# New slots and engines for the elementwise work of an attention-plus-Mish block

## The chip, the cores and the metric

The kernel runs on one core of a Trainium2 chip. The metric is the device time of one execution in microseconds (us), lower is better. Before the change it is 1112.99 us, the median of three runs (1112.70 to 1113.39).

The engines of a core are named as the profile does: PE is TensorE (matmuls; PEld is its weight load), DVE is VectorE, ACT is ScalarE, POOL is GpSimd, and SP issues the transfers (DMAs). Each engine runs its own instructions in program order and waits at semaphores for the others.

## The reference

```python
def _A_ref(x, wqkv, wo):          # S=2048 tokens, D=576, 32 heads of 18
    q, k, v = ...                 # x @ wqkv
    idx = pos[:, None] - (jnp.arange(8) * 2)[None, :]   # 8 keys: the token and every second before it
    logits = jnp.einsum("bhsd,bhswd->bhsw", q, kg) * scale
    attn = _softmax(jnp.where(mask, logits, -1e9), axis=-1)
    o = jnp.einsum("bhsw,bhswd->bhsd", attn, vg)
    return o.transpose(...).reshape(B, S, D) @ wo

def _B_ref(x, w1, b1, w2):        # F=4608
    h = jnp.einsum("bsd,df->bsf", x, w1) + b1
    act = h * jnp.tanh(stable_softplus(h))               # Mish
    return jnp.einsum("bsf,fd->bsd", act, w2)

xn = _layernorm(x)
return x + _A_ref(xn, A_wqkv, A_wo) + _B_ref(xn, B_w1, B_b1, B_w2)
```

Everything is float32. The attention is a sliding window of eight dilated keys, so it has no large matmul: its products of queries with keys and of weights with values are elementwise.

## The kernel before

The 2048 tokens are worked in two halves of 1024 (`hf` 0 and 1). A half goes through these matmul stages on TensorE: the layernormed tokens transposed (`ta`, `tb`), the query-key-value product (`pq`, L424, and the `z` items, L594), for each of 18 blocks of the hidden width the first MLP product with Mish (`h`, L826 and L832, in six parts), and the second MLP product (`po`: L948 in the first half, as products named P1 to P7 by L1084 and L1100 in the second). At the end comes the output product (`o`, L1230). Every float32 operand is split into two pieces, "high" (a rounded copy, mostly made by ScalarE) and "low" (the difference, an elementwise subtraction), and a product takes three matmuls: high·high, high·low, low·high. The matrices are also multiplied in schemes of seven products in place of eight on 2×2 blocks, which need sums and differences of blocks ahead (`tt`, `S`, `ra`, `rm`, `v`, `wa`), each split into high and low again. This is the elementwise work that fills VectorE and GpSimd:

- low parts: `t`, `w`, `wa`, `wc`, `wq` (L271), `u` and `ud` (L1007), `act` (L893), `v` (L384);
- block sums: `w1_sum` `tt` (L256), `v_sum` (L376), `wa` (L302), `u_sum` (L994);
- taking results out of PSUM, which GpSimd never reads: `h` in L882, `acc` in L952, `accP` in L1106, `zqs` in L607;
- the attention (L677 and on): a half has 8 pairs (`n` is half_pair). For each pair `pr` = query times window of keys (L699), VectorE reduces it (L704), softmax (L714 to L730), `pv` = weights times values (L737), VectorE reduces it into `og` (L743), and the last reduce's result is stored. Each `pr` and `pv` product comes as two instructions of 128×576, with the keys `pr half_pair k c x` and `pv half_pair k h x`. `pr` and `pv` share one tag of two buffers.

The order of all work is written out by hand. A list of TensorE items, `plan`, gives the rows of a timeline, six slots to an item; matmuls stand in slot 4. Every piece of elementwise work and every transfer is put into the slot that `before` or `soon` work out from the item that it is for, moved by a table of numbers:

```python
def put(pos, fn, key):
    pos += MOVE.get(key, 0)
    assert pos > now[0], key
    timeline[pos].append(fn)

def engine(default, *key):
    k = " ".join(str(x) for x in key)
    return nc.vector if k in ON_VECTOR else nc.gpsimd if k in ON_GPSIMD else default
```

The attention runs as a generator, one step of it in each slot named `att n`. The timeline is then gone through slot by slot, and the instructions of each engine are chained in that order. So three tables decide, for each engine, which instruction stands behind which: `MOVE` (how many slots earlier or later), `ON_VECTOR` and `ON_GPSIMD` (which engine, where it is not the default). `pr` and `pv` are GpSimd's by default; the low parts of L271 VectorE's; those of `u` some of each.

## Time and profile before

| what | value |
|---|---|
| median of 3 runs | 1112.99 us (1112.70 to 1113.39) |
| the profiled execution, its own time | 1111.6 us |
| its span in the profile | 1109.7 us |
| granted TensorE clock | 1.000 |
| busy: PE, DVE, POOL, ACT | 1088.6, 976.2, 770.8, 532.8 us |
| moved by DMA | 290.51 MB, 262 GB/s mean |

The span runs from the first instruction to the last. The 1.9 us between it and the execution's own time lie outside what the profile shows. Busy times of engines overlap. "A <- B" in the view of waits means that A stood idle until B was done.

### The profile page before, as it was taken

How to read it: one execution, taken by the hardware profiler on the slowest of the kernel's cores; microseconds unless marked ns; L12 is line 12 of the kernel's file. 1: busy time of each engine (PE TensorE's matmuls, PEld its weight loads, DVE VectorE, ACT ScalarE, POOL GpSimd, SP SyncE). 2: the span in 40 equal slices, each digit the busy share in tenths (PEclk: the TensorE clock that was granted, in tenths of full speed). 3: DMA queues.
4: the chain of work that ended last, by engine and by line, in shares of the span. 5: the costliest groups of instructions: out<-in, count | busy, mean ns of one | idle time of the engine just before them, and what ended most of it. 6: DMA issues, size and time to landing. Idle time of an engine off the chain costs nothing.

```text
span 1109.7 us, 18409 instructions
## 1 busy us (share of the span) xinstructions
PE 1088.6 (98%) x6414; PEld 993.4 (90%) x6414; DVE 976.2 (88%) x1580; ACT 532.8 (48%) x984; POOL 770.8 (69%) x595
## 2 busy tenths in 40 slices
PE   8999999999999999999999999999999999999998
PEld 7898999899989988799999888888988899989998
DVE  7843899998998988998877899999999999998886
ACT  5644656546555545863233364354444344434332
POOL 5342668785677878768657477776988878896652
PEclk9999999999999999999999999999999999999999
DMA  8698999897799879877597798557565668675772
GB/s 272 220 334 260 326 317 310 280 326 261 268 315 340 313 284 359 302 232 270 183 313 242 252 357 270 197 205 236 184 233 188 253 213 298 223 265 179 276 224 93
DMA packets 171377, 290.51 MB, mean 262 GB/s; under 512 B 32242, under 2 KB 107284, under 8 KB 171284
## 3 DMA queue, kind: packets, MB, share of 16 engines
q1 hardware_dynamic: 171284, 289.33, 75.7%
q8 instruction: 51, 0.84, 0.3%
q14 instruction: 42, 0.34, 0.1%
HBM read 179.05 MB, written 110.23 MB: 261 GB/s over the span
## 4 chain that ended last, share of the span: by engine, by line
PE 62%; DVE 16%; POOL 9%; issue 5%; ACT 4%; DMA 3%; SPq 0%; POOLq 0%; DVEq 0%; ACTq 0%
PE h L826 18%; PE po L1100 9%; PE po L948 9%; PE pq L424 6%; PE z L594 6%; PE pd L1084 5%; PE o L1230 4%; PE h L832 4%; POOL pr L699 3%; POOL pv L737 2%; DVE pv L737 2%; DVE og L743 2%; POOL u L1007 1%; DVE accP L1106 1%; DVE acc L952 1%
## 5 line engine op out<-in xcount | busy, mean ns | idle before, releaser
L1100 PEld LDWEIGHTS po<-pw,u 128*128 128x128 f32 x1512 | 207.6, 188 | 13.9 <-POOL u L1007 3.1
L1100 PE MATMUL po<-pw,u 128*128 128x288 f32 x1512 | 214.2, 296 | 5.3 <-DVE accP L1106 2.0
L948 PEld LDWEIGHTS po<-w,act 128*128 128x128 f32 x1152 | 157.7, 188 | 5.5 <-DVE acc L952 1.5
L948 PE MATMUL po<-w,act 128*128 128x288 f32 x1152 | 160.8, 295 | 0.7 <-DVE acc L952 0.7
L737 POOL TENSOR_TENSOR pv<-L,kv 128x576 f32<-128x576 f32 x85 | 133.6, 1649 | 35.6 <-ACT zkv L603 9.1
L699 POOL TENSOR_TENSOR pr<-q,kv 128x576 f32<-128x576 f32 x89 | 144.7, 1644 | 13.7 <-DVE og L743 12.5
L826 PE MATMUL h<-xt,t 128*128 128x512 f32 x432 | 111.2, 393 | 2.8 <-DVE rd_raw L882 1.5
L826 PE MATMUL h<-S,t 128*128 128x512 f32 x432 | 110.6, 391 | 0.0
L826 PE MATMUL h<-xt,wa 128*128 128x512 f32 x432 | 105.3, 392 | 0.0
L1106 DVE TENSOR_TENSOR accP<-po,accP 128x288 f32<-128x288 f32 x240 | 94.8, 445 | 6.5 <-PE po L1100 6.2
L826 PEld LDWEIGHTS h<-xt,wa 128*128 128x128 f32 x432 | 81.1, 188 | 18.0
L826 PEld LDWEIGHTS h<-xt,t 128*128 128x128 f32 x432 | 79.1, 188 | 20.1 <-DVE rt L882 2.0
L424 PE MATMUL pq<-wq,xt 128*128 128x432 f32 x448 | 92.0, 361 | 1.9 <-ACT xt L96 1.1
L826 PEld LDWEIGHTS h<-S,t 128*128 128x128 f32 x432 | 78.5, 188 | 14.3 <-ACT rd_a L871 0.3
L424 PEld LDWEIGHTS pq<-wq,xt 128*128 128x128 f32 x448 | 83.0, 188 | 7.4 <-ACT xt L96 1.8
L704 DVE TENSOR_REDUCE L<-pr 128x64 f32<-128x1152 f32 x64 | 85.8, 1341 | 3.1 <-POOL pr L699 2.8
L743 DVE TENSOR_REDUCE og<-pv 128x144 f32<-128x1152 f32 x64 | 85.8, 1342 | 0.8 <-POOL pv L737 0.4
L952 DVE TENSOR_TENSOR acc<-po,acc 128x288 f32<-128x288 f32 x192 | 77.1, 446 | 10.5 <-PE po L948 10.2
L737 DVE TENSOR_TENSOR pv<-L,kv 128x576 f32<-128x576 f32 x43 | 63.0, 1495 | 0.4
L1084 PE MATMUL pd<-pd,ud 128*128 128x288 f32 x456 | 62.5, 296 | 0.0
L1084 PEld LDWEIGHTS pd<-pd,ud 128*128 128x128 f32 x456 | 61.2, 188 | 0.4 <-DVE acc L1089 0.2
L826 PE MATMUL h<-S,wc 128*128 128x512 f32 x216 | 55.8, 394 | 0.6 <-ACT c L871 0.4
(340 smaller groups left out, 2275.4 us busy)
## 6 DMA issues: line engine op xcount, KB each, us to landing
kv<-kv_d SPq DMA_DIRECT2D x64, 396.0 KB, 5.4
pw<-kept_T SPq DMA_DIRECT2D x36, 576.0 KB, 5.8
kept_t<-t SPq DMA_DIRECT2D x36, 512.0 KB, 5.5
t<-kept_t SPq DMA_DIRECT2D x36, 512.0 KB, 4.8
pw<-kept_B SPq DMA_DIRECT2D x27, 576.0 KB, 4.2
rw<-in_w SPq DMA_DIRECT2D x36, 320.0 KB, 5.0
kept_B<-w SPq DMA_DIRECT2D x36, 288.0 KB, 4.8
kept_wq<-wq SPq DMA_DIRECT2D x18, 432.0 KB, 6.0
```

Source lines behind the costliest of these rows:

```text
L424: nc.tensor.matmul(pq[:, 0:432], XT[:, xi, tok], wt[wi][:, hl, 0:432], start=i == 0, stop=i == len(seq) - 1)
L594: nc.tensor.matmul(h, l, r_, start=first and n == 0, stop=n == len(seq) - 1, skip_group_check=True)
L699: engine(nc.gpsimd, "pr", n, k, c, x).tensor_tensor(out=pr[:, x:x + hh], in0=q[:, j0 + x:j0 + x + hh, None, :].to_broadcast([P, hh, W, CU] ...
L704: nc.vector.tensor_reduce(L[:, k, j0:j0 + hj].rearrange("p j w h -> p (j w h)"), pr.rearrange("p j w (h d) -> p (j w h) d", h=2), axis=AX, ...
L737: engine(nc.gpsimd, "pv", n, k, h, x).tensor_tensor(out=pr[:, x:x + hj].rearrange("p j d w -> p j w d"), in0=L[:, k, x:x + hj, :, h:h + 1] ...
L743: nc.vector.tensor_reduce(og[:, :, c0:c0 + DH], pr, axis=AX, op=ALU.add)
L826: nc.tensor.matmul(ph, wt[:, wl, wk * P:(wk + 1) * P], X[:, xs, :], start=first and i == 0, stop=last and i == len(seq) - 1, skip_group_ch ...
L948: nc.tensor.matmul(po, acts[hf, q, b, j][:, al, tok], done["w2", hf, 2 * q + j][:, wl, c * HC:(c + 1) * HC], start=i == 0, stop=i == 5)
L952: nc.vector.tensor_tensor(out=t, in0=po, in1=t, op=ALU.add)
L1084: nc.tensor.matmul(po, units[e, k, qq][:, al, n * P:(n + 1) * P], w[qq][:, wl, :], start=i == 0, stop=i == 5)
L1100: nc.tensor.matmul(po, units[e, k, qq][:, al, tok], w[:, qq, wl, :], start=i == 0, stop=i == 5)
L1106: nc.vector.tensor_tensor(out=t, in0=po, in1=t, op=ALU.add)
```

## The change

Three lines change, all of them literal tables. `MOVE` goes from 1910 keys to 1918, and 1820 of the 1978 keys in either have another value; half of the differences are of six slots (one item) or less, the largest of 136. `ON_VECTOR` gains 106 keys and loses 77 (273 to 302), `ON_GPSIMD` gains 48 and loses 43 (145 to 150). In the diff the lines are cut to some of the keys that are spoken of below, one to a line:

```diff
 MOVE = {
...
-"act 0_1_4": 15, "act 0_1_5": 15,
+"act 0_1_4": 18, "act 0_1_5": 12,
...
-"att 60": 1, "first 1": -13, "low t0 4": -10, "low t1 3": -9, "low w2 6": -5,
+"att 60": -8, "first 1": 16, "low t0 4": -19, "low t1 3": 2, "low w2 6": -12,
...
-"u_low 1 0 0": 21, "u_low 1 0 1": -3, "u_low 1 1 0": -37, "u_low 1 1 1": 10,
+"u_low 1 0 0": 23, "u_low 1 0 1": -2, "u_low 1 1 0": -24, "u_low 1 1 1": -7,
...
 ON_VECTOR = (
...
-"pv 0_4 1 1 0", "pv 0_4 1 1 4", "pv 0_5 1 1 0", "pv 0_5 1 1 4", "pv 0_7 0 0 0", "pv 0_7 0 0 4",
-"pv 0_7 1 0 0", "pv 0_7 1 1 4", "u_low 1 2 0",
+"act 0_1_5", "pv 0_7 0 1 0", "pv 0_7 1 0 4", "u_low 1 0 0", "u_low 1 1 0", "u_low 1 1 1",
...
 ON_GPSIMD = (
...
-"low t0 4", "low t1 3", "low w2 6",
+"u_low 1 0 1",
...
```

What the tables do to the engines, by their instructions in order: TensorE has the same 6416 instructions; a group of three transposes for the output product stands one P item earlier, the rest is as before. ScalarE keeps 986 and SP its 860 transfers, in another order. VectorE goes from 1582 to 1606, GpSimd from 600 to 576. By kind, net to VectorE: −22 `pv` (11 in each half), +14 `pr` (9 and 5), +16 `u_low`, +8 `w1_sum`, +7 `t` and +4 `v_sum`, +2 `v_low`, and a few of others either way.

**First place: VectorE at the end of pair 5 of the first half's attention**, where the second half's first MLP block begins. `rt0` and `ra0` are taken from PSUM (L882). Before:

```order
L743 TENSOR_REDUCE og_0_5_7359<-pv_0_5_0_1_7425 128x8x18
L737 TENSOR_TENSOR pv_0_5_1_0_7433<-L_0_5_7157,kv1_0_11_7178 128x4x8x18
L743 TENSOR_REDUCE og_0_5_7359<-pv_0_5_1_0_7433 128x8x18
L737 TENSOR_TENSOR pv_0_5_1_1_7446<-L_0_5_7157,kv1_0_11_7178 128x4x8x18 x2
L882 TENSOR_TENSOR rt0_7407<-h3_1_0_7438,rt0_7407 128x512
L882 TENSOR_TENSOR ra0_7398<-h2_1_0_7410,ra0_7398 128x512
L743 TENSOR_REDUCE og_0_5_7359<-pv_0_5_1_1_7446 128x8x18
```

And with the change:

```order
L743 TENSOR_REDUCE og_0_5_7339<-pv_0_5_0_1_7364 128x8x18
L737 TENSOR_TENSOR pv_0_5_1_0_7399<-L_0_5_7133,kv1_0_11_7206 128x4x8x18
L302 TENSOR_TENSOR wa_1_2_7115<-wraw_1_7116,wa_1_2_7115 128x640
L743 TENSOR_REDUCE og_0_5_7339<-pv_0_5_1_0_7399 128x8x18
L882 TENSOR_TENSOR rt0_7420<-h3_1_0_7439,rt0_7420 128x512
L882 TENSOR_TENSOR ra0_7411<-h2_1_0_7423,ra0_7411 128x512
L743 TENSOR_REDUCE og_0_5_7339<-pv_0_5_1_1_7458 128x8x18
```

The last two `pv` instructions of the pair have left VectorE, and one sum `wa` has come in. At the same point of pair 4, ahead of a `zqs` evacuation, two `pv` have left too.

**Second place: VectorE between taking out the products P3 (`accP3`) and P7 (`accP7`)**, in the second half's P items, where the first half's attention pair 7 ends. Before:

```order
L737 TENSOR_TENSOR pv_0_7_0_0_8085<-L_0_7_7900,kv1_0_14_7906 128x4x8x18 x2
L882 TENSOR_TENSOR ra_r_7950<-h3_1_3_7937,ra_r_7950 128x512
...
L1106 TENSOR_TENSOR accP3_1_7485<-po_0_6_1_1_8114,accP3_1_7485 128x288
L994 TENSOR_TENSOR ra_r_7950<-ra0_7398,ra_r_7950 128x512
L743 TENSOR_REDUCE og_0_7_8084<-pv_0_7_0_0_8085 128x8x18
L1007 TENSOR_TENSOR u_1_0_1_8163<-ra_r_7950,u_1_0_1_8163 128x512
L743 TENSOR_REDUCE og_0_7_8084<-pv_0_7_0_1_8168 128x8x18
L737 TENSOR_TENSOR pv_0_7_1_0_8182<-L_0_7_7900,kv1_0_15_7935 128x4x8x18
L743 TENSOR_REDUCE og_0_7_8084<-pv_0_7_1_0_8182 128x8x18
L737 TENSOR_TENSOR pv_0_7_1_1_8186<-L_0_7_7900,kv1_0_15_7935 128x4x8x18
L1106 TENSOR_TENSOR accP7_0_7676<-po_1_0_0_0_8189,accP7_0_7676 128x288
```

And with the change:

```order
L1007 TENSOR_TENSOR u_1_1_0_7919<-rt0_7420,u_1_1_0_7919 128x512
...
L1106 TENSOR_TENSOR accP3_1_7453<-po_0_6_1_1_8106,accP3_1_7453 128x288
L882 TENSOR_TENSOR ra0_7411<-h2_1_3_7929,ra0_7411 128x512
L882 TENSOR_TENSOR ra_r_7960<-h3_1_3_7941,ra_r_7960 128x512
L994 TENSOR_TENSOR ra_r_7960<-ra0_7411,ra_r_7960 128x512
L1007 TENSOR_TENSOR u_1_0_0_8078<-rm0_7415,u_1_0_0_8078 128x512
L1007 TENSOR_TENSOR u_1_1_1_8117<-rt1_7421,u_1_1_1_8117 128x512
L743 TENSOR_REDUCE og_0_7_8066<-pv_0_7_0_0_8067 128x8x18
L737 TENSOR_TENSOR pv_0_7_0_1_8158<-L_0_7_7911,kv1_0_14_7917 128x4x8x18
L743 TENSOR_REDUCE og_0_7_8066<-pv_0_7_0_1_8158 128x8x18
L737 TENSOR_TENSOR pv_0_7_1_0_8172<-L_0_7_7911,kv1_0_15_7952 128x4x8x18
L1106 TENSOR_TENSOR accP7_0_7683<-po_1_0_0_0_8177,accP7_0_7683 128x288
```

Ahead of P3's evacuation the two `pv` and the `ra_r` evacuation have gone and a `u` stands there; between P3's and P7's, two evacuations and one `u` more, one reduce less, and `u_1_0_1` is no longer VectorE's.

**Third place: VectorE in the first half's block 2**, up to the low part `act_0_1_4` for the second MLP product. Before:

```order
L704 TENSOR_REDUCE L_0_0_1315<-pr_0_0_1_1_1675 128x64
...
L384 TENSOR_TENSOR v0_12_1651<-v0_12_1651,vh0_12_1795 128x576
L882 TENSOR_TENSOR c21_0_2_1747<-h3_0_2_1684,c21_0_2_1747 128x512
...
L336 TENSOR_TENSOR twT2_2_1734<-twT2_2_1734,twhT2_2_1897 128x576
L326 TENSOR_TENSOR twT3_3_1958<-rw2_7_1757,rw2_6_1867 128x288
L326 TENSOR_TENSOR twT3_3_1958<-rw2_6_1867 128x288
L384 TENSOR_TENSOR v2_12_1691<-v2_12_1691,vh2_12_1942 128x576
L384 TENSOR_TENSOR v3_12_1813<-v3_12_1813,vh3_12_1869 128x288
L893 TENSOR_TENSOR act_0_1_4_1901<-c21_0_2_1747,act_0_1_4_1901 128x512
```

And with the change:

```order
L384 TENSOR_TENSOR v0_12_1398<-v0_12_1398,vh0_12_1824 128x576
L271 TENSOR_TENSOR t1_0_3_1816<-tt1_3_1644,t1_0_3_1816 128x512
L704 TENSOR_REDUCE L_0_0_1281<-pr_0_0_1_1_1528 128x64
...
L893 TENSOR_TENSOR act_0_1_5_1828<-c22_0_2_1814,act_0_1_5_1828 128x512
...
L882 TENSOR_TENSOR c21_0_2_1753<-h3_0_2_1682,c21_0_2_1753 128x512
L271 TENSOR_TENSOR w2_0_6_1862<-rw2_6_1734,w2_0_6_1862 128x576
L384 TENSOR_TENSOR v2_12_1649<-v2_12_1649,vh2_12_1946 128x576
L271 TENSOR_TENSOR t0_0_4_1889<-tt0_4_1818,t0_0_4_1889 128x512
L893 TENSOR_TENSOR act_0_1_4_1943<-c21_0_2_1753,act_0_1_4_1943 128x512
```

Two `t`, a `w2` and an `act`, GpSimd's before, stand now on VectorE ahead of `act_0_1_4`, and four rows of preparation have moved elsewhere.

6 lines of the change are left out of this document (3 added, 3 removed).

## The prediction, before the changed kernel was run

> **What bounds the kernel now.** I read the engines' busy shares first. TensorE (PE) works for almost the whole span, so the time is its 1088.6 us plus what it waits: 1109.7 − 1088.6 = 21.1 us.
>
> ```profile
> span 1109.7 us, 18409 instructions
> ...
> PE 1088.6 (98%) x6414; PEld 993.4 (90%) x6414; DVE 976.2 (88%) x1580; ACT 532.8 (48%) x984; POOL 770.8 (69%) x595
> ```
>
> Since the order of TensorE's instructions hardly changes, the change can act only on those 21.1 us. Next, therefore, the view of waits for PE alone (who waited, for whom; us in total, times, longest); three rows of 0.4, 0.2 and 0.2 are left out:
>
> ```profile
> PE po L1100 <- DVE accP L1106: 2.0, 1, 2.0
> PE po L1100 <- POOL u L1007: 1.6, 4, 0.7
> PE ta L90 <- ACT xn L195: 1.5, 2, 0.9
> PE h L826 <- DVE rd_raw L882: 1.5, 1, 1.5
> PE tb L93 <- POOL rem L209: 1.4, 1, 1.4
> PE warm L80 <- POOL ident masks.py:199: 1.3, 1, 1.3
> PE pq L424 <- ACT xt L96: 1.1, 2, 0.6
> PE h L826 <- DVE rt L882: 1.1, 2, 0.7
> PE tb L91 <- DVE xt L97: 0.9, 1, 0.9
> PE po L1100 <- ACT u L1000: 0.9, 1, 0.9
> PE po L1100 <- DVE u L1007: 0.7, 1, 0.7
> PE po L948 <- DVE acc L952: 0.7, 2, 0.4
> PE z L594 <- DVE zqs L607: 0.7, 1, 0.7
> PE o L1230 <- DVE y L1234: 0.6, 1, 0.6
> PE pq L424 <- DVE xt L97: 0.5, 1, 0.5
> ...
> ```
>
> All rows come to 17.3 us; the rest is gaps too short for a row and about 3 us behind the last matmul. No row names a DMA. I split the sum in two. **Fixed**: the start and the layernorm transposes (warm, ta, tb, the pq rows: 1.5 + 1.4 + 1.3 + 1.1 + 0.9 + 0.5 + 0.2 = 6.9) with the 0.2 of a row left out, and the 1.5 of rd_raw, 8.4 in all; the instructions ahead of these waits stand in the same order in the changed kernel. **Movable**: the other rows, 8.9 us. So without new waits the best that the change could do is −8.9.
>
> Two stages of the table by stage tell where there is room for new ones (window, length, then PE, PEld, DVE, ACT and POOL busy, clock, DMA share, GB/s):
>
> ```profile
> 112.00:448.00 336.00, 335.31 (x1945) 301.16 (x1944) 310.31 (x507) 188.01 (x313) 245.01 (x199) 1.00 0.89 307
> ...
> 640.00:1026.00 386.00, 381.18 (x2233) 342.43 (x2232) 370.48 (x544) 178.64 (x289) 310.57 (x210) 1.00 0.67 235
> ```
>
> The clock is 1.00 throughout. VectorE (DVE) is the second bound: in the first long stretch it has 336 − 310.3 = 25.7 us of slack and TensorE waits only 0.7; in the second VectorE has 386 − 370.5 = 15.5 and TensorE waits 4.8.
>
> **The change, part by part.** First what the moved work costs on each engine, from the groups (busy us, mean ns of one):
>
> ```profile
> L737 POOL TENSOR_TENSOR pv<-L,kv 128x576 f32<-128x576 f32 x85 | 133.6, 1649 | 35.6 <-ACT zkv L603 9.1
> L699 POOL TENSOR_TENSOR pr<-q,kv 128x576 f32<-128x576 f32 x89 | 144.7, 1644 | 13.7 <-DVE og L743 12.5
> ...
> L743 DVE TENSOR_REDUCE og<-pv 128x144 f32<-128x1152 f32 x64 | 85.8, 1342 | 0.8 <-POOL pv L737 0.4
> L737 DVE TENSOR_TENSOR pv<-L,kv 128x576 f32<-128x576 f32 x43 | 63.0, 1495 | 0.4
> L699 DVE TENSOR_TENSOR pr<-q,kv 128x576 f32<-128x576 f32 x39 | 37.8, 979 | 0.0
> L1007 DVE TENSOR_TENSOR u<-ra,u 128x512 fp32r<-128x512 f32 x32 | 29.8, 936 | 1.8 <-ACT u L1000 1.8
> L1007 POOL TENSOR_TENSOR u<-rm,u 128x512 fp32r<-128x512 f32 x31 | 44.3, 1431 | 13.4 <-ACT u L1000 13.4
> L271 DVE TENSOR_TENSOR t<-tt,t 128x512 fp32r<-128x512 f32 x24 | 18.3, 766 | 0.8 <-ACT t L270 0.7
> ```
>
> VectorE: 22 pv leave (−22 × 1.495 = −32.9), 14 pr come (+13.7), 16 low parts of u come (+15.0), 7 of t come (+5.4): +1.2, and with some forty smaller moves about +3 on 976. GpSimd: +36.3 − 23.0 − 22.9, and about −26 on 771 with the rest. Totals decide nothing here, as both engines keep slack; places do. Per pv the move frees 1.5 us of VectorE for 1.65 of GpSimd, and per pr it costs VectorE 0.98 and frees 1.64: as an exchange it is a good one by these rows.
>
> The Trainium skill, GPSIMD Engine Reference, section 4.1 "Engine selection", sends elementwise work on a tile to VectorE, since GpSimd is about 2 times slower with two inputs; that speaks against the 22 pv. The rows disagree for this shape (1649 against 1495 is 1.10 times) and come nearer for pr (1.68) and u (1.53); by the page's factor the 22 would cost GpSimd an estimated 22 × 2 × 1.495 = 65.8 us in place of 36.3, which its slack of some 340 us would still take.
>
> Now the places, by the timeline (start, us, engine, line, count; in brackets the wait and its releaser):
>
> ```profile
> 593.31 3.63 DVE L737 TENSOR_TENSOR pv<-L,kv 128x576 f32<-128x576 f32 x2
> ...
> 601.91 1.44 PE L594 MATMUL z<-z_B,S 128*128 128x432 f32 x6 [0.66 <-DVE zqs L607]
> ...
> 628.07 3.60 DVE L737 TENSOR_TENSOR pv<-L,kv 128x576 f32<-128x576 f32 x2
> 631.52 0.67 DVE L882 TENSOR_TENSOR rt<-h,rt 128x512 f32<-128x512 f32 x1
> ...
> 632.25 1.66 PE L826 MATMUL h<-xt,t 128*128 128x512 f32 x6 [0.72 <-DVE rt L882]
> ...
> 689.74 1.92 PE L1100 MATMUL po<-pw,u 128*128 128x288 f32 x13
> ...
> 691.34 3.46 DVE L737 TENSOR_TENSOR pv<-L,kv 128x576 f32<-128x576 f32 x2
> 695.23 1.54 DVE L1106 TENSOR_TENSOR accP<-po,accP 128x288 f32<-128x288 f32 x4
> 699.37 2.81 PE L1100 MATMUL po<-pw,u 128*128 128x288 f32 x19 [0.68 <-DVE u L1007]
> 703.17 2.07 DVE L737 TENSOR_TENSOR pv<-L,kv 128x576 f32<-128x576 f32 x1
> 705.10 1.52 DVE L1106 TENSOR_TENSOR accP<-po,accP 128x288 f32<-128x288 f32 x4
> 705.59 0.66 PE L1100 MATMUL po<-pw,u 128*128 128x288 f32 x3 [2.05 <-DVE accP L1106]
> ```
>
> (1) **The seam, 593 to 633.** A pair of pv, 3.6 us long, stands on VectorE ahead of the evacuations for which TensorE waits, zqs and rt. Both (of attention pairs 4 and 5; the first place shown of VectorE's order is the second of them) go to GpSimd. Ahead of rt one sum of L302 comes in, which I bound by the 1.5 of a pv. That leaves the evacuations over 2 us earlier against waits of 0.66 and 0.72, so both waits go: **−1.4** (bounds −1.4 and 0). What is late next is the reduce of that pv, which feeds only a store and later attention work.
>
> (2) **Pair 7, 691 to 706.** TensorE had the four P3 products ready by 689.74 + 1.92 = 691.66, but VectorE takes them out only at 695.23, behind two pv; the row of rows that follows keeps P7's evacuation until 705.10, and TensorE waits 2.05. Now one u_low (0.94) stands in the pv's place: the evacuation can begin at 691.34 + 0.94 = 692.3 and ends at 693.8. From its end to P7's it was 705.10 − 696.77 = 8.33; in the new order two plain evacuations and a u_low come in (0.67 each, as the row at 631.52, and 0.94) and a reduce leaves (1.34), +0.95. P7 then begins at 693.8 + 9.3 = 703.1, 2.0 earlier.
>
> But u_1_0_1, the cause of the 0.68, now goes to GpSimd, and the reduces between must wait for GpSimd too, 2 × 1.649 = 3.3 for a pair behind what it is doing, so I take not the whole 2.05 + 0.68 = 2.73 but **−1.5** (bounds −2.7 and +0.5).
>
> (3) **The other movable waits of the second half**: 8.9 − 1.4 − 2.7 = 4.8, mostly u on GpSimd (1.6) and ScalarE (0.9). Sixteen u_low go to VectorE at 0.94 in place of 1.43, but get new neighbours. With the places of most of them reset either way I take **−0.5** (bounds −3 and +2).
>
> (4) **The first long stretch, 112 to 448.** Pricing VectorE's new order by the group means, its work there grows by 11.4 us (six t, six w1 sums, four v sums and four pr come, five pv leave): slack falls from 25.7 to 14.3, or 4.3% of 336. That is the share at which VectorE works in the second stretch (15.5 of 386, 4.0%), where TensorE waits 4.8 in 386, or 4.2 per 336. So the price lies between 0 and 4.2 − 0.7 = +3.5. The third place shown is one of these: two moved t, a moved w and a moved act_0_1_5 stand now ahead of act_0_1_4, and four rows of preparation went away. I take **+1.0**, nearer the low end, as most rows here fill matmuls that come later.
>
> (5) **Fixed waits and the tail**: 0. ScalarE's work is the same, SP issues the same transfers in another order, and no PE wait names a transfer.
>
> Sum: −1.4 − 1.5 − 0.5 + 1.0 = −2.4. The profiled execution took 1111.6 with its span of 1109.7; the span becomes 1107.3. The median of before lies 1112.99 − 1109.7 = 3.3 above that span, so the forecast is **1110.6**, own range 1108.5 to 1112.2.
>
> **The rivals.** *A larger gain* (14%): by the same freeing of VectorE, (3) goes to its end, −3, and (4) to 0: with −2.9 of (1) and (2) it is −5.9, 1107. For it speaks that every movable wait stands behind VectorE or GpSimd; against it, that u waits come from orders which are merely reset.
>
> *No change* (22%): VectorE's reduces of pv wait now on GpSimd, which does both halves of more pv in a row (3.3 us) where the two engines had shared them, and whatever follows them there is late again; (1) stays, (2) and (3) come to 0 and (4) to +1.0: −0.4, 1112.6. The row of pv that took 2.07 against a mean of 1.495, while GpSimd was busy, speaks for it. The Trainium skill, SBUF — State Buffer, section "SBUF: two separate sides", has VectorE operations with two SBUF inputs and GpSimd exclude each other; by it an exchange between the two engines gains no time at all, and that 2.07 is the only sign of it quoted here.
>
> *Slower* (14%): the queue of the first stretch. If VectorE's work in 112 to 448 exceeds about 326 of 336 us, low parts of act come late one after the other, since each stands behind one or two added rows (0.77 to 1.54): act_0_1_4, act_0_0_7, act_0_1_10 and act_0_1_12 stand so in the new order. Four times 1.5 is +6 and, against −3.4 of (1) to (3), +2.6 in all: **1116** (with (2) at its upper bound, +0.5, 1118). Against it speaks the slack of 14 us.
>
> *A late transfer* (8%): SP issues in order, and its DMAs are reset. The issues of the weights for the P products (KB each, median us to landing):
>
> ```profile
> pw<-kept_T SPq DMA_DIRECT2D x36, 576.0 KB, 5.8
> ```
>
> One miss costs at most about that; with −2.4 it is some +3, also 1116. No wait of before names a transfer.
>
> **How the numbers follow.** The forecast has 42%. Changes under 0.2%, 2.2 us, cannot be told from none; the forecast lies just beyond that edge, so its 42 split into 26 faster and 16 same. Faster: 26 + 14 = 40%. Same: 16 + 22 = 38%. Slower: 14 + 8 = 22%. The range takes in the larger gain and the slower case with their spread: 1105 (the floor is 1112.99 − 8.9 = 1104.1) to 1118.
>
> **What would show it.** In the profile after: no rows zqs and rt of 0.7 at the seam (1); an accP wait under 1 (2); POOL u waits about 1 (3); VectorE busy in 112 to 448 near 321 and PE waits there of 1 to 2 (4); fixed rows as they are (5). A PE row that names a DMA, or PE waits over 3 in the first long stretch, would prove it wrong.

## The result, and the profile after

The changed kernel takes 1103.11 us (median of 4 runs, 1102.19 to 1103.32) against 1113.19 of the kernel before on the same chip: a ratio of 0.9907, 95% interval 0.9890 to 0.9925, or −10.1 us. On another chip it was 1102.46 against 1112.84, 0.9908 [0.9892, 0.9924]. The forecast was 1110.6, with 1105 as the lower end of its range. The direction was right and the size was not. One execution each of `engines`, `gp_tt`, `from36` (the profiled one, at a granted clock of 0.56) and, on the other chip, of the kernel before ran far longer than the rest; the medians given here count them, the ratios and intervals leave them out.

The profiled execution took 1102.98 us, its span is 8.5 us shorter than that of before. The rest of the 10.1 is the profiled execution of before, which at 1111.6 was 0.8 to 1.8 below the medians of its kernel in the comparisons of this document. The head of the page after, busy time by engine:

```profile
span 1101.2 us, 18382 instructions
...
PE 1086.5 (99%) x6414; PEld 995.8 (90%) x6414; DVE 960.5 (87%) x1604; ACT 532.3 (48%) x984; POOL 738.4 (67%) x571
```

VectorE has 24 instructions more than before and is 15.7 us less busy (976.2 to 960.5). The prediction had it at +3. Such a number can differ by some 5 us where next to nothing changed: two executions of the change give 960.5 and 961.8, but a kernel that differs from before in one slot only (`mish35`, experiment 6) gives 971.4 where before gives 976.2. GpSimd has 32.4 us less to do (770.8 to 738.4), where the prediction had −26. Next, TensorE's waits after (who waited for whom; us in total, times, longest):

```profile
PE ta L90 <- ACT xn L195: 2.1, 1, 2.1
PE tb L93 <- POOL rem L209: 1.4, 1, 1.4
PE warm L80 <- POOL ident masks.py:199: 1.3, 1, 1.3
PE po L1100 <- DMA pw<-kept_T: 1.2, 2, 0.7
PE pq L424 <- ACT xt L96: 1.2, 2, 0.6
PE o L1230 <- DVE accP L1234: 0.8, 1, 0.8
PE po L1100 <- ACT oa L1166: 0.6, 1, 0.6
PE h L826 <- ACT rm L871: 0.6, 1, 0.6
PE h L826 <- DMA t<-kept_t: 0.6, 1, 0.6
PE po L1100 <- DVE accP L1106: 0.5, 1, 0.5
PE h L826 <- DVE rt L882: 0.5, 1, 0.5
PE pd L1084 <- DVE acc L1089: 0.2, 1, 0.2
```

The rows come to 11.0 where before's came to 17.3. Of those by which VectorE or GpSimd held TensorE up in the second MLP product (accP, u) only 0.5 is left. The rd_raw row, which the prediction called fixed, is gone. Two DMA rows are new, 1.8 in all (the prediction had named a DMA row as a sign of being wrong); a second execution of the change (`after_again`) has only 0.2 of them. The first row has grown by 0.6.

The stages after (window, length, then PE, PEld, DVE, ACT and POOL busy, clock, DMA share, GB/s):

```profile
112.00:448.00 336.00, 336.00 (x1953) 302.79 (x1953) 306.37 (x528) 190.07 (x315) 221.60 (x181) 1.00 0.89 309
...
640.00:1026.00 386.00, 383.04 (x2272) 346.66 (x2272) 366.12 (x558) 179.12 (x290) 301.25 (x206) 1.00 0.68 241
```

In the first long stretch VectorE works 306.4 us and not the 321 that the prediction gave as its mark, with 21 instructions more than before. GpSimd's work there fell from 245.0 to 221.6.

Since a window of fixed times holds other work in the two kernels, the stages are compared by TensorE's instructions: the time from the first to the last of the same matmuls, before and after. "Gaps" is the listed idle time among them; the rest is stalls too short to be listed and matmuls that run closer.

| same matmuls, by times of before | before, us | change | of it gaps | change, other chip | forecast |
|---|---|---|---|---|---|
| 0 to 112 | 110.78 | +0.40 | −1.31 | +1.73 | 0 |
| 112 to 448 | 335.90 | −1.85 | −0.69 | −1.64 | +1.0 |
| 448 to 640 | 192.16 | −2.41 | −2.20 | −2.79 | −1.4 |
| 640 to 1026 | 385.82 | −4.43 | −2.37 | −5.62 | −2.0 |
| 1026 to the end | 80.23 | −0.24 | +0.19 | −0.25 | 0 |

A stage of one execution is uncertain by 1 to 1.5 us: in two of the experiments below whose kernels keep the time of before, 112 to 448 came out at −1.0 and −1.1, and 640 to 1026 at +1.5 and −0.3. So the first long stretch is read as "did not get longer", and the gain as lying in the seam and above all in the second half.

**Where VectorE's time went.** For each VectorE instruction I took the time from the end of the one before it (or its own start) to its end, and sorted the instructions by whether GpSimd was working beside them (over 90% of their time, or under 10%). Mean us, with counts, of before and after:

```
                                   before: alone   beside       after: alone   beside
L1007 u    two inputs in SBUF      0.608 (38)  1.085 (27)       0.608 (40)  1.096 (28)
L271       two inputs in SBUF      0.606 (32)  1.119 (21)       0.599 (38)  1.138 (18)
L699 pr    two inputs in SBUF      0.666 (10)  1.058 (18)       0.667 (18)  0.947 (22)
L737 pv    two inputs in SBUF      1.214 (12)  1.478 (24)       1.345  (1)  1.268 (16)
L743       a reduce, one input     1.280  (5)  1.269 (55)       1.263  (4)  1.267 (52)
L882       one input in PSUM       0.604 (15)  0.606 (82)       0.624 (12)  0.612 (82)
L1106      one input in PSUM       0.365 (11)  0.373 (215)      0.401 (23)  0.380 (202)
```

Rows that read two operands from SBUF take on average 1.2 to 1.9 times as long beside GpSimd before (`pv` 1.2, `pr` 1.6, `u` 1.8, L271, whose tiles are of several widths, 1.9); reduces and rows that read PSUM do not notice it. The timeline of VectorE after shows it in one place (start, us):

```profile
734.63 1.34 DVE L743 TENSOR_REDUCE og<-pv 128x144 f32<-128x1152 f32 x1
735.89 1.69 DVE L1007 TENSOR_TENSOR u<-rm,u 128x512 fp32r<-128x512 f32 x1
737.77 1.40 DVE L1007 TENSOR_TENSOR u<-rt,u 128x512 fp32r<-128x512 f32 x1 [0.20 <-ACT u L1000]
739.10 1.68 DVE L994 TENSOR_TENSOR rm<-rt,rm 128x512 f32<-128x512 f32 x1
740.70 1.77 DVE L994 TENSOR_TENSOR ra<-ra,rm 128x512 f32<-128x512 f32 x1
742.40 1.54 DVE L1106 TENSOR_TENSOR accP<-po,accP 128x288 f32<-128x288 f32 x4
743.86 0.81 DVE L302 TENSOR_TENSOR wa<-wraw,wa 128x640 fp32r<-128x640 f32 x1
744.59 0.68 DVE L1007 TENSOR_TENSOR u<-ra,u 128x512 fp32r<-128x512 f32 x1
```

and GpSimd's at the same time:

```profile
731.73 8.64 POOL L737 TENSOR_TENSOR pv<-L,kv 128x576 f32<-128x576 f32 x6 [0.58 <-issue]
740.21 1.71 POOL L1007 TENSOR_TENSOR u<-rt,u 128x512 fp32r<-128x512 f32 x1
```

Until GpSimd stops at 741.92, a `u` takes 1.40 to 1.69; behind it, 0.68. The reduce at 734.63 takes its 1.34 all the same. Summed over all two-input rows, the time above the lone duration (the **excess**) was 108.7 us before and is 90.9 after, −17.8, while the same rows at their lone durations come to 300.1 and 299.1. So the drop of VectorE's busy time is the excess. It is not simply that GpSimd has 32 us less to do: `engines` of experiment 1, which has the change's engines with the places of before, leaves GpSimd as short and VectorE with the same 1604 instructions, and yet VectorE is longer than before:

```profile
PE 1102.8 (96%) x6414; PEld 996.4 (87%) x6414; DVE 985.8 (86%) x1604; ACT 532.9 (46%) x984; POOL 736.3 (64%) x571
```

So the excess goes by which rows stand beside which, and engines and places set that together.

### The profile page after: what moved, and what is told of

Its sections match the earlier page's. It is cut to its first block, busy times and chain, and to the rows that moved or that the text cites. A ratio compares the mean times of both kernels' runs of the same rounds, so it can differ in the third digit from the quotient of the medians.

```text
span 1101.2 us, 18382 instructions
## 1 busy us (share of the span) xinstructions
PE 1086.5 (99%) x6414; PEld 995.8 (90%) x6414; DVE 960.5 (87%) x1604; ACT 532.3 (48%) x984; POOL 738.4 (67%) x571
## 4 chain that ended last, share of the span: by engine, by line
PE 85%; DVE 5%; DMA 3%; POOL 3%; issue 2%; ACT 1%; SPq 0%; ACTq 0%; DVEq 0%; POOLq 0%
PE h L826 28%; PE po L1100 15%; PE po L948 14%; PE z L594 7%; PE pq L424 6%; PE h L832 5%; PE pd L1084 5%; PE o L1230 4%; DMA pw<-kept_T 2%; POOL pr L699 1%; DMA acc<-in_x 1%; DMA t<-kept_t 1%; DVE u L1007 1%; POOL pv L737 1%; DVE og L743 0%
## 5 line engine op out<-in xcount | busy, mean ns | idle before, releaser
L737 POOL TENSOR_TENSOR pv<-L,kv 128x576 f32<-128x576 f32 x107 | 162.6, 1612 | 46.0 <-DVE L L730 29.7
L699 POOL TENSOR_TENSOR pr<-q,kv 128x576 f32<-128x576 f32 x75 | 124.5, 1672 | 21.1 <-DVE og L743 10.2
L424 PE MATMUL pq<-wq,xt 128*128 128x432 f32 x448 | 93.3, 365 | 1.3 <-ACT xt L96 1.2
L826 PEld LDWEIGHTS h<-S,t 128*128 128x128 f32 x432 | 78.4, 188 | 15.7 <-issue 1.0
L424 PEld LDWEIGHTS pq<-wq,xt 128*128 128x128 f32 x448 | 84.1, 191 | 6.9 <-ACT xt L96 1.8
L699 DVE TENSOR_TENSOR pr<-q,kv 128x576 f32<-128x576 f32 x53 | 47.1, 904 | 1.8 <-DMA q<-q_d 1.8
```

The source lines that it names most:

```text
L424: nc.tensor.matmul(pq[:, 0:432], XT[:, xi, tok], wt[wi][:, hl, 0:432], start=i == 0, stop=i == len(seq) - 1)
L699: engine(nc.gpsimd, "pr", n, k, c, x).tensor_tensor(out=pr[:, x:x + hh], in0=q[:, j0 + x:j0 + x + hh, None, :].to_broadcast([P, hh, W, CU] ...
L737: engine(nc.gpsimd, "pv", n, k, h, x).tensor_tensor(out=pr[:, x:x + hj].rearrange("p j d w -> p j w d"), in0=L[:, k, x:x + hj, :, h:h + 1] ...
L826: nc.tensor.matmul(ph, wt[:, wl, wk * P:(wk + 1) * P], X[:, xs, :], start=first and i == 0, stop=last and i == len(seq) - 1, skip_group_ch ...
```

## The experiments

The question was which part of the change brings the time: VectorE's shorter list, GpSimd's, the smaller excess, or the slots. Changes to the tables are shown by some of their keys, with the number of keys that differ.

**1. One table without the other.** `slots` has the change's slots and the engines of before (only `low t1 3`, which would otherwise stand too late, takes its default engine); `engines` has the opposite; `att_engines` moves only the `pr` and `pv` entries of ON_VECTOR (41 out, 33 in) in the slots of before; `slots_att` adds the change's slots to that (with three `low t1` entries of GpSimd left out).

```diff
 MOVE = {
...
-"act 0_1_4": 15, "act 0_1_5": 15,
+"act 0_1_4": 18, "act 0_1_5": 12,
...
 ON_VECTOR = (
...
-"pv 0_4 1 1 0", "pv 0_4 1 1 4", "pv 0_5 1 1 0", "pv 0_5 1 1 4",
+"act 0_1_5", "pv 0_7 0 1 0", "pv 0_7 1 0 4",
```

> The slots of the change with the engines of before (all entries but one low part of t1). Theory A (the order of the queues makes the gain, each row at its price): about 1106, with the waits on zqs, rt and accP7 back in part since the pv stay on VectorE. Theory B (VectorE's rows with two SBUF inputs become shorter because GpSimd has 32 us less to do): at least 1110, since GpSimd's work is that of before. Under both the wait on rd_raw is gone, because the slots alone set it.

> The engines of the change with the slots of before. Theory A: 1112 to 1118, because the order of VectorE's queue does not fit the new engines and the wait on rd_raw stays. Theory B: 1105 to 1108, with VectorE busy near 960 us in place of 976.

> Slots of before; of the engines only those of the attention's products (22 pv to GpSimd, 14 pr to VectorE, net). Theory A: the two pv pairs at the seam and those of pair 7 are gone from VectorE, so the waits on zqs, rt and accP7 (3.4 us) are mostly gone and nothing else: 1109.5. Theory B: VectorE loses a net 19 us of work and its rows shorten a little: 1107 to 1109. If the reduces wait on GpSimd instead, 1113 or above.

> Slots of the change and the engines of its attention products; all other engines of before (but one low part of t1). Theory A: 1104, as the change, within 1.5. Theory B: 1107 to 1109, since the 16 u_low and the other small moves that relieve GpSimd are missing (GpSimd busy about 805 in place of 738).

Measured against 1112.44: `slots` 1183.37, 1.0617 [1.0587, 1.0647]; `engines` 1149.31, 1.0317 [1.0297, 1.0337]; `att_engines` 1127.10, 1.0127 [1.0109, 1.0144]; `slots_att` 1165.64, 1.0479 [1.0458, 1.0500]. Every part is a loss, of 15 to 71 us, and together they gain 10. That missed nearly all of what was expected: theory A is out by far in all four, and of theory B only the bound for `slots` (at least 1110) holds; `att_engines` is in the third case, 1113 or above, far beyond its bound. The wait for rd_raw, expected to go wherever the slots are the change's, is still there in `slots` (2.8 us) and `slots_att` (3.4). The loss of `att_engines` lies in the second half (+12.8 of its stages). There TensorE's waits, 4.8 before, are (longest four):

```profile
PE po L1100 <- DVE u L1007: 4.9, 6, 1.3
PE h L826 <- DVE rt L882: 2.1, 4, 0.7
PE po L1100 <- POOL u L1007: 1.8, 4, 0.6
PE h L826 <- DVE rm L882: 1.6, 1, 1.6
```

TensorE waits more for VectorE there. Over the span VectorE is 7.6 us less busy than before (968.6), but not in this stage: beside the same matmuls it is 375.0 us busy with 537 instructions where before had 370.6 with 544, as the excess of its rows there is about 15 us higher. VectorE also waits in this stage for GpSimd's `pv`, 2.8 us. Experiment 3 asks how much of the loss is GpSimd's lateness. In the old slots the move is bad.

**2. Leaving work out, on each engine in turn.** In the kernel before, 22 of GpSimd's `pv` products are replaced by a fill with zeros (`gp_less`), spread over all pairs, or 22 of VectorE's (`dve_less`), all of them among the 30 that the change takes off VectorE, those ahead of zqs, rt and accP included; the weighted values are therefore not computed in full. A fill takes 0.54 to 0.60 us, where a `pv` took 1.5 to 1.65.

```diff
-                        engine(nc.gpsimd, "pv", n, k, h, x).tensor_tensor(
+                        if left_out("pv", n, k, h, x):
+                            engine(nc.gpsimd, "pv", n, k, h, x).memset(pr[:, x:x + hj], 0.0)
+                        else:
+                            engine(nc.gpsimd, "pv", n, k, h, x).tensor_tensor(
```

> The kernel before, in its own order; 22 of GpSimd's pv products (k 1, h 0, all pairs and both halves) are left out and replaced by a memset of the same tile on GpSimd, so those weighted values are missing. GpSimd loses 22 x (1.65 - 0.58) = 23.5 us of work, about what the change takes from it, and reads SBUF 36 us less. Theory C (what counts is how long VectorE's rows with two SBUF inputs lie beside GpSimd's): VectorE's busy time falls by some 14 us with the same instructions and the time by 4 to 8. Theory V (VectorE's own list of work): within 1.5 of before. Theory O (only the new order, places for places): within 1.5 of before.

> The kernel before, in its own order; 22 of VectorE's pv products (of those that the change moves away) are left out and replaced by a memset of the same tile on VectorE, so those weighted values are missing. VectorE loses some 22 us, GpSimd none. Theory V: the waits on zqs, rt, u and accP7 behind pv go, time -4 to -8. Theory C: VectorE's other rows are as long as before and GpSimd as late; only the four places of the forecast gain, -3. Theory O: -2 or less, since the freed time stands where nothing waits for it.

Measured against 1113.35: `gp_less` 1112.86, 0.9995 [0.9985, 1.0006]; `dve_less` 1103.95, 0.9917 [0.9902, 0.9931]. Their busy times, first of `gp_less`:

```profile
PE 1091.2 (98%) x6414; PEld 996.8 (90%) x6414; DVE 968.2 (87%) x1580; ACT 533.0 (48%) x984; POOL 748.9 (67%) x595
```

then of `dve_less`:

```profile
PE 1087.3 (99%) x6414; PEld 994.4 (90%) x6414; DVE 945.6 (86%) x1580; ACT 533.5 (48%) x984; POOL 753.9 (68%) x595
```

This points at the lever. Taking 21.9 us off GpSimd leaves the time as it was, though VectorE is also 8.0 less busy (excess 108.7 to 100.1, of which up to 5 can be the spread between executions). Taking these `pv` rows off VectorE brings 9.4 us, more than the 4 to 8 that theory V had and nearly the gain of the change, and 5.9 of its 7.6 us of span lie in 640 to 1026, where the listed gaps fall from 4.83 to 0.29. So the theory that less excess, wherever it stands, brings the gain falls: what counts is which rows stand ahead of the evacuations and low parts for which TensorE waits. GpSimd, of which nothing was taken, is 16.9 us less busy in `dve_less` (770.8 to 753.9, a `pv` there 1.55 us on average in place of 1.65); the expectation had it at none. So the two engines lengthen each other's rows, and work taken off VectorE is worth more than its own length. In `dve_less` the wait for rd_raw still stands (the line numbers are 8 higher there):

```profile
PE h L834 <- DVE rd_raw L890: 1.5, 1, 1.5
```

**3. Why `att_engines` loses what `dve_less` gains.** `att_gpless` is `att_engines` with 27 of GpSimd's `pv` products replaced by the fill as above.

> The slots of before with the engines of the attention's products of the change (as att_engines, which took 1127.1), and 27 of GpSimd's pv products (k 1, h 0) left out and replaced by a memset on GpSimd, so those weighted values are missing; GpSimd loses some 28 us. If att_engines lost because GpSimd takes on 22 pv at places where it has no room and VectorE's reduces wait for it: 1104 to 1112, most of the loss gone. If it lost because of VectorE's new rows (14 pr) at places that don't fit: above 1120.

Measured against 1112.84: 1118.18, 1.0049 [1.0033, 1.0065]. The loss falls from 14.7 to 5.3, which lies between the two cases of the expectation. About two thirds of the loss therefore hang on GpSimd's load in the old slots. In which way is not shown: GpSimd's products are less late (VectorE's wait for `pv` in 640 to 1026 falls from 2.8 to 1.5 us), but VectorE is also 10 us less busy there than in `att_engines`, with 27 fewer products beside it. The rest may be VectorE's 14 new `pr` rows and their places, which this does not split further.

**4. The change with GpSimd loaded again.** In pairs 1, 2 and 3 of the first half, whose work lies in the first long stretch, `gp_tt` makes 12 of GpSimd's `pr` and `pv` products twice; `gp_set` puts three fills ahead of each of the 12 instead (36 × 0.58 us).

```diff
+    def more(kind, n, *key):
+        return n in ("0_1", "0_2", "0_3") and engine(nc.gpsimd, kind, n, *key) is nc.gpsimd and key[-1] == 0
...
-                        engine(nc.gpsimd, "pv", n, k, h, x).tensor_tensor(
+                        for _ in range(2 if more("pv", n, k, h, x) else 1):
+                          engine(nc.gpsimd, "pv", n, k, h, x).tensor_tensor(
```

> The changed kernel, with 12 of GpSimd's products of the first half's pairs 1 to 3 (112 to 470 us) made twice with the same result: some 20 us more of GpSimd, about what the change had taken away there. Theory C (VectorE's rows with two SBUF inputs are longer while GpSimd reads SBUF): VectorE gets 7 to 10 us busier in 112 to 448 with not one instruction more, and the time grows by 2 to 6. Theory Q (only GpSimd's own lateness counts, 336 - 222 us of it idle): VectorE as in the change, time +0 to +1.5.

> The changed kernel with three memsets on GpSimd ahead of each of the same 12 products, into the tile that the product then fills: GpSimd busy for a like time, but reading nothing from SBUF. Theory C: VectorE's rows stay as in the change (within 2 us in 112 to 448), time +0 to +1. Theory Q: the same loss as with the products made twice. If any write of GpSimd slows VectorE too, VectorE grows here as well.

Measured against 1112.85: `gp_tt` 1109.89, 0.9974 [0.9964, 0.9983]; `gp_set` 1107.32, 0.9950 [0.9937, 0.9963]. That is 6.8 and 4.2 more than the change at 1103.11 (1102.46 on the other chip); theory C had 2 to 6 and 0 to 1, theory Q at most 1.5 for `gp_tt`, so both miss the time. The same matmuls of 112 to 448 take 340.6 and 337.6, against 334.1. The groups of `gp_set`'s fills (busy us, mean ns):

```profile
L743 POOL MEMSET pv<- 128x576 f32 x21 | 12.2, 580 | 0.8
L703 POOL MEMSET pr<- 128x576 f32 x15 | 8.7, 580 | 0.6
```

GpSimd works 22.5 and 23.1 us more in the two; the excess of VectorE grows by 8.1 and 3.9. So products that read SBUF make VectorE's rows longer by roughly a third of a us per us, here as in `gp_less` (8.0 per 21.9); the 3.9 of the fills is not clear of the spread between executions. The trace of `gp_tt` accounts in part for the 6.5 us by which its stretch is longer. It has a wait for GpSimd's own lateness that the change has not:

```profile
PE po L953 <- POOL act L898: 1.7, 1, 1.7
```

It costs 1.9 us from start to start of the same matmuls, and the granted clock is half for the 3.4 us behind it, another 1.5 (14 matmuls, each 0.11 longer). Waits for VectorE's `act` and `acc` that the change has not come to some 1.6; the rest is in small pieces. So excess is at most a part of the 6.8. In the new order the room on GpSimd is used up: a like amount of work, some 22 us, which taken off was worth nothing in the order before, costs 4 to 7 when put on here.

**5. Transplants in time.** Keys of work that belongs to a stretch of TensorE's items come from the change, the others from before: `from262` from 641 us on (744 slots differ from before), `to262` up to there (1076), `first_only` the items of about 112 to 448 us (674), `from36` all but the first 36 items (1690). `after_again` is the change itself.

```diff
 MOVE = {
...
-"u_low 1 0 0": 21, "u_low 1 0 1": -3,
+"u_low 1 0 0": 23, "u_low 1 0 1": -2,
```

> The changed kernel with the tables of before for the first 36 items of TensorE's plan (up to 103 us). In the profile of the change the time up to 112 us is 0.4 us longer than before, with a wait of 2.1 us for xn; if stages stand by themselves, this wait is that of before again and the kernel is 0.4 faster than the change: 1102.7. If what starts early decides what follows, over 1106.

> The kernel before with the tables of the change (slots and engines together) for items 36 to 184, 103 to 448 us, alone. If slots and engines belong together by the stretch, this one gives what it gave in the change, -1.85 us between 112 and 448: 1110.6, with VectorE busy there near 306 in place of 310 and no wait on rd_raw or zqs gone. If only the whole tables fit: slower than 1114. By my own sum of the forecast (+1.0): 1113.5.

> The kernel before, with the change's slots and engines together from item 262 of the plan on (641 us to the end) and before's ahead of it. If the gain belongs to the stages, the second half gives what it gave in the change, -4.4 in 640 to 1026 us and -0.2 behind: 1108.5. If only the whole tables fit: slower than 1114.

> The complement: the change's slots and engines up to item 262 (641 us), before's behind it. Stage by stage in the change: +0.4 up to 112, -1.85 in 112 to 448, -2.4 in 448 to 640, together -3.9: 1109.3. If only the whole tables fit: slower than 1114.

> The changed kernel once more, beside the others on one chip: 1103, as before; its profile tells how far one profile of it differs from the next.

Measured: `from262` 1107.76 against 1112.84, 0.9954 [0.9936, 0.9971], with −3.8 in 640 to 1026; `to262` 1110.46, 0.9982 [0.9971, 0.9993], with −2.5 in 448 to 640 and +1.7 in 0 to 112; `after_again` 1102.46. The parts, −5.1 and −2.4, come to −7.5 of −10.4; the 2.9 between is not explained. So about half of the gain belongs to the second half's tables alone. That fits `from262` (expected 1108.5) and `to262` (1109.3). `from36` (1111.26 against 1112.85, 0.9986 [0.9976, 0.9996]) came out in the second case of its expectation, some 8 us above the change with all but the first 36 items its own, and `first_only` (1121.02, 1.0075 [1.0062, 1.0088]) missed the 1110.6. Both say little about the stretches: in `first_only` the cut made a wait of its own,

```profile
PE h L826 <- ACT c L871: 7.3, 1, 7.3
```

and +8.3 of its time lie ahead of 112 us, where ScalarE's cast of `w` ahead of that copy waits 7.7 us for a store (0.4 before); no stages could be read of `from36`. In `first_only`'s own stretch the same matmuls take +0.3, no more than a stage of one execution is uncertain by.

**6. Single steps of the prediction.** `seam_pv` moves only the seam's four `pv` rows of step (1) to GpSimd in the order before; `mish35` sets one slot, so that rd_raw stands earlier.

```diff
-"pv 0_4 1 1 0", "pv 0_4 1 1 4", "pv 0_5 1 1 0", "pv 0_5 1 1 4",
```

```diff
-"mish 0_1_35": 14,
+"mish 0_1_35": 4,
```

> The kernel before with four pv instructions moved to GpSimd, the pairs of pv 0_4 1 1 and pv 0_5 1 1 ahead of zqs and rt, and nothing else. My step (1) by itself: the two waits of 0.7 us go, -1.4 to -1.7: 1111.2. If GpSimd's next work (the query-key products and the sums s behind it) comes 3.3 us later each time and is waited for: 1113 or above.

> The kernel before with one number of its slot table changed: the Mish of block 35 (0_1_35) at 4 in place of 14, as in the change, so that rd_raw is taken out ahead of the second transposed tile's copies. Theory O: the wait of 1.5 us on rd_raw at 464 us goes, and with it 1.5 us of the time: 1111.3. If the wait only moves on: no change, and another wait of 1 to 1.5 stands in the 30 us behind it.

Measured against 1113.35: `seam_pv` 1111.59, 0.9988 [0.9977, 0.9999]; `mish35` 1112.58, 0.9994 [0.9985, 1.0003]. In `seam_pv` the two waits of 0.7 become 0.2 and 0.3:

```profile
PE h L826 <- DVE rt L882: 0.3, 1, 0.3
PE z L594 <- DVE zqs L607: 0.2, 1, 0.2
```

and 448 to 640 gets 0.6 shorter; step (1)'s mechanism holds. In `mish35` the 1.5 for rd_raw is gone, but within the next 6 us a new wait stands,

```profile
PE pd L1084 <- DVE ud L1007: 0.8, 1, 0.8
```

and the matmuls are back at their old distance after it and a smaller one for `daccP`. So a wait that is taken away alone moves on. In the change 0.6 of the 1.5 came back by 491 us and 0.9 did not; that this is because the rows behind it have moved too is likely, but no run shows it.

**7. A sum of the start.** The change also gives `f_sum T4`, a sum of 128×864 (L477) of the preparation, to GpSimd. `fsum_eng` is the change with that one entry back on VectorE; `fsum_moved` is the kernel before with it on GpSimd.

```diff
 ON_VECTOR = (
...
+"f_sum T4",
```

> The changed kernel with one entry set back: the sum f_sum T4 (L477, 128x864) on VectorE, where it stands behind the layernorm's nm, in place of GpSimd. In the change, GpSimd's L477 ran to 29.88 us and VectorE's row of 128x2 at 28.29 (L132, 0.16 us elsewhere) ended with it, at 29.91. If that row waits for GpSimd's instruction to end (an exclusive lock): 0.16 us for the row, xn 1.5 us earlier, the wait of 2.1 us on xn at 0.6, and 1.5 to 2.5 us less: 1101.0. If it waits for something else that ends by chance at the same time: L132 still 1.6 us and no change, 1102.5 to 1103.

> The reverse, the kernel before with the same one entry as in the change: f_sum T4 on GpSimd. With the lock: L132 takes 1.6 us in place of 0.16, the wait for xn grows by about 1.5, and what lies behind keeps it: 1114.3. Without: 1112.8, or less, since VectorE does one sum less.

Measured against 1113.23: `fsum_eng` 1101.70, 0.9896 [0.9879, 0.9913]; `fsum_moved` 1112.79, 0.9991 [0.9982, 1.0001]. The change, by the timelines of VectorE, GpSimd and TensorE in turn:

```profile
28.29 1.62 DVE L132 TENSOR_TENSOR y<-rs 128x2 f32<-128x2 f32 x1 [0.51 <-ACT rs L175]
```

```profile
25.46 4.42 POOL L477 TENSOR_TENSOR fraw<-fraw,fraw 128x864 f32<-128x864 f32 x2
```

```profile
33.99 0.66 PE L90 MATMUL ta<-ident,xn 128*128 128x128 f32 x4 [2.13 <-ACT xn L195]
```

and `fsum_eng`, VectorE and TensorE:

```profile
27.89 0.16 DVE L132 TENSOR_TENSOR y<-rs 128x2 f32<-128x2 f32 x1 [0.51 <-ACT rs L175]
```

```profile
32.15 0.66 PE L90 MATMUL ta<-ident,xn 128*128 128x128 f32 x4 [0.59 <-ACT xn L195]
```

A row of two elements per partition, 0.16 us long, ends at 29.91, when GpSimd's second sum ends (29.88): 1.46 us late, and the layernorm behind it makes TensorE wait 2.13 in place of 0.59. With the entry back this is gone, but another wait of 1.7 (pq for a low part of `xt` from VectorE) appears, and the median, though the lowest of all kernels here, cannot be told from the change's: the intervals of the two ratios overlap. In `fsum_moved` the sum came later, met other rows, and nothing was lost. So what such a row costs depends on where it stands beside GpSimd's rows.

## Why the prediction was right and wrong

**What bounds the kernel.** Right: the change acted on TensorE's waits, and VectorE was in the main what held it up; `dve_less` shows it by experiment. Wrong: the split into fixed and movable waits, and with it the floor of 1104.1. The rd_raw wait of 1.5 was said to have the same instructions ahead of it. It has not: before, L882 of rd_raw stands behind both transposed tiles' copies (L97, L102), after it stands between them. Before:

```profile
463.76 0.69 DVE L882 TENSOR_TENSOR rd_raw<-h,rd_raw 128x512 f32<-128x512 f32 x1
...
464.51 1.66 PE L826 MATMUL h<-xt,t 128*128 128x512 f32 x6 [1.51 <-DVE rd_raw L882]
```

After, no wait stands at the same matmuls:

```profile
460.44 0.69 DVE L882 TENSOR_TENSOR rd_raw<-h,rd_raw 128x512 f32<-128x512 f32 x1
...
461.19 1.66 PE L826 MATMUL h<-xt,t 128*128 128x512 f32 x6
```

That is −1.5 at this place, which the order would have shown. The floor also took a wait for its listed length. Each of four waits that went saved some 0.16 us more than its row: 0.66 gave 0.82, 0.72 gave 0.88, 0.68 gave 0.84 and 2.05 gave 2.21, from start to start of the same matmuls; rd_raw's 1.51 gave 1.49. And some 2 us of the second half's gain is in stalls too short for a row.

**(1) The seam, −1.4.** Right: −0.82 and −0.88, −1.7 in all. A transfer that is late, new at 633.5 (`t` from kept_t), gives back 0.8 in this execution and nothing in `after_again`.

**(2) Pair 7, −1.5.** Right in its mechanism, too small: −0.84 (u), −2.21 (accP) and a new wait for a transfer (`pw`, the one that the late-transfer rival named) of +0.71, together −2.3; `after_again` gets +0.28 for it and −2.8 in all. I kept 1.2 back because `u_1_0_1` and GpSimd's pairs of `pv` might come late; they did not:

```profile
696.68 1.54 DVE L1106 TENSOR_TENSOR accP<-po,accP 128x288 f32<-128x288 f32 x4
```

This is P7's evacuation, 8.4 us earlier than before's 705.10, of which 4.5 had been gained ahead of this place.

**(3) The other waits of the second half, −0.5.** Too small. The whole stage gave −4.4 and −5.6, so −2.1 and −2.9 are left behind (2). The step failed in treating the reset of the places as a coin toss about nothing, while its own rows said that each `pv` taken off frees VectorE 1.5 us in the stage where TensorE waits for it; `dve_less` got −5.9 there with no new order at all.

**(4) The first long stretch, +1.0.** Wrong in sign and, with the second half, the largest miss of a stage: −1.9 and −1.6, at least no loss. The failing step is the pricing of VectorE's new order by the group means of before, +11.4 us. A group's mean is made of rows beside GpSimd at 1.1 and rows alone at 0.6, and the change alters how many there are of each. In this stretch the rows at their lone durations grew by 7.1 (108.3 to 115.4), the excess fell by 12.8 (44.9 to 32.1), and its other rows add some 1.8. VectorE's work went down by 3.9 where I let it go up by 11.4. In the stretch GpSimd lost 23 us of work and the rows got new places; how much of the 12.8 each brought, no run separates. `gp_tt` is a counter-check in part: GpSimd's work put back in the stretch brought 8.1 of excess and 6.5 us of time, of which some 3.4 are GpSimd's own late `act` and the clock behind it.

**(5) Fixed waits and the tail, 0.** Wrong by rd_raw above, and at the start, which lost 0.4 and 1.7; the sum of experiment 7 has a part in that (`fsum_eng` has −0.3 there), and in `after_again` waits for `pq` add to it.

**The rivals.** "No change" rested on the two engines excluding each other. The exclusion is real, but I gave it the wrong consequence. The Trainium skill, SBUF — State Buffer, section "SBUF: two separate sides", has the pair of ports held for a whole instruction, by a GpSimd operation on one side and on the other by a VectorE operation with two SBUF inputs (there only against a GpSimd operation that reads SBUF) or in a 2-port performance mode. The L132 row, held until GpSimd's end, agrees, and so do the reduces and PSUM rows that are not slowed at all. By that rule an exchange pays if it lowers the number of such meetings, as the change did (excess −17.8) and the same moves in the old places did not (`engines`, VectorE +9.6), and I read it as "gains nothing". The "larger gain" was the right side and still too small, at 1107, since it used the same floor. The "slower" queue in the first stretch did not form.

**What stays open.** How the 10 us divide between fewer rows on VectorE and better places for the rest: no experiment changes the one without the other, since both tables alone lose. Less excess over the whole span brought nothing in the order before (`gp_less`); whether it would where TensorE waits is open. Of GpSimd's load in `att_engines`, lateness and longer rows are not told apart. The 2.9 us by which the two halves of the transplant fall short are not explained.

## What to carry to other kernels

Price a moved elementwise row by what runs beside it at its place, alone or beside GpSimd, and not by its group's mean, which already holds the contention that the change may remove. Before judging a rebalancing, leave the work out on each engine in turn: here 22 products off GpSimd were worth nothing and 22 others off VectorE 9 us, which points at the engine whose list has to get shorter. Slots and engines of one schedule are one thing: the engines alone lost 37 us and the slots alone 71, so a part tried by itself does not tell what it is worth in the whole.

## What was not expected of the hardware

**A tiny row can wait for a whole large one.** Beside the L132 row, the start of the kernel before holds another: a row with one SBUF input (L173), which takes 0.16 us a little later.

```profile
25.51 2.02 DVE L173 TENSOR_SCALAR ve<-mv 128x2 f32<-128x2 f32 x1
...
30.06 0.16 DVE L173 TENSOR_SCALAR ve<-mv 128x2 f32<-128x2 f32 x1
```

At the same time GpSimd has

```profile
25.20 2.30 POOL L477 TENSOR_TENSOR fraw<-fraw,fraw 128x864 f32<-128x864 f32 x1
```

and both end at 27.5. This wait of 1.9 us is in both kernels and in all other traces but one: in that of `from36` GpSimd's two sums end at 30.3 and the row comes at 32.20, with GpSimd idle, and takes 0.16. That the row is long because GpSimd's sum stands beside it fits this and the L132 row; nothing was changed to test it.

**The clock can fall behind a short wait.** Behind the 2.13 us wait of the change, the granted clock in the window 30 to 40 us is 0.83 (columns as in the stages; the clock is third from the end):

```profile
30.00:40.00 10.00, 7.80 (x37) 6.79 (x36) 5.37 (x17) 6.90 (x19) 2.42 (x5) 0.83 0.01 3
```

The same window before:

```profile
30.00:40.00 10.00, 8.37 (x45) 7.00 (x44) 7.34 (x14) 8.23 (x22) 6.43 (x10) 1.00 0.29 92
```

Behind the wait seven matmuls of L424 run at 0.36 us from start to start and not 0.20, and one in part, about 1.3 us in all. With a wait of 0.59 in that place (`fsum_eng`) the clock stays at 1.00. But length alone does not decide it: `gp_set` has a wait of 2.07 in the same place and keeps its clock,

```profile
30.00:40.00 10.00, 7.59 (x41) 6.23 (x40) 5.39 (x17) 8.55 (x21) 2.44 (x6) 1.00 0.10 32
```

while in `gp_tt` it falls both here (2.06) and behind the 1.7 us of experiment 4. So a wait of about 2 us can cost 1.3 to 1.5 us more than its length, and did in some executions. The profile of before shows no fall, but of the 90 executions that were measured of it beside the experiments 40 have a mean granted clock of 0.998 and 50 of 1.000, at 1113.8 and 1112.5 us on average. What decides it these traces do not show.

**Whether fills on GpSimd slow VectorE is open.** The fills read nothing, and 20.9 us of them came with 3.9 us more excess. Two kernels that differ in one slot differ by 4.8 us in VectorE's busy time, and the products behind the fills came to stand beside other rows; the runs do not tell these apart.
